# The last output tile of an attention and MLP kernel in two column pieces of 384 and 128

## The chip, the cores and the metric

The kernel runs on one core of one Trainium2 chip. The metric is the time of one execution on the device in microseconds.

## The reference

```python
scores = 0.125 * q @ k_all^T            # 8 batches, 8 heads, 576 queries, 16 beacon + 576 keys, D = 64
a = softmax(causal mask of scores)      # the beacon keys are always seen
x = (a @ v_all) as 4608 tokens x 512
h = x @ w_in                            # 512 -> 2048
g = h * sigmoid(1.702 * h)
out = g @ w_out                         # 2048 -> 512, float32, 4608 x 512
```

## The kernel before

The program is a list of work items, which a small scheduler orders when the program is built. The MLP takes the tokens in nine groups of 512. The second matrix product of a group makes four output tiles of 128 tokens by 512 columns. Each is 16 accumulating matmuls, a copy from PSUM to SBUF, and a store:

```python
def mlp2(g, mt):
    o = psu.tile([P, DMODEL], F32, tag="u", name="u")
    ou[(g, mt)] = o
    for nt in range(NNT):                                  # 16
        nc.tensor.matmul(o[:, :], gts[g][:, nt, mt * P : (mt + 1) * P], w2t[:, nt, :],
                         start=(nt == 0), stop=(nt == NNT - 1))

def mlp2_out(g, mt, eng):
    osb = sp.tile([P, DMODEL], F32, tag="osb", name="osb")
    ...                                                    # nc.scalar.copy or nc.vector.tensor_copy
    ou[(g, mt)] = osb

def mlp2_store(g, mt):
    t0 = g * GT + mt * P
    nc.sync.dma_start(out=out[t0 : t0 + P, :], in_=ou[(g, mt)][:, :])
```

The pool psu has four buffers in PSUM, the pool of osb three in SBUF.

The softmax here doesn't subtract the row's maximum and nothing guards it: scores larger than these inputs give would overflow.

## Time and profile before

| | before |
|---|---|
| time | 367.96 us (three runs, 367.85 to 367.99) |
| span of the profiled run | 366.9 us |
| start of the last tile's first matmul, called T | 359.55 us |
| last copy starts | T + 3.65 |
| last store issued | T + 4.37 |
| its last completion count | T + 6.38 |
| end of the span | T + 7.31 |

T and the times from it are read off the trace's records of single instructions, packets and completion counts. A completion count is what a store adds to a semaphore when a part of it is done: 16 counts for each store here. A store has landed with its last count, and the time from the end of its last data packet to that count is called its receipt. Stores take eight such semaphores in turn, numbered 0 to 7. At the end of the program SP, the engine that issues the stores, waits for them in a fixed order: these are the closing waits.

Two stretches, before and after the end of the last matmul, show how little there is to win:

```profile
core 0: us, PE busy (x) PEld busy (x) DVE busy (x) ACT busy (x) POOL busy (x), PEclk, DMA share, GB/s
359.30:363.20 3.90, 3.87 (x18) 1.57 (x16) 0.69 (x1) 0.00 (x0) 0.00 (x0) 1.00 0.18 67
363.20:367.00 3.80, 0.00 (x0) 0.00 (x0) 0.69 (x1) 0.00 (x0) 0.00 (x0) 0.96 0.18 69
```

In the first, TensorE is busy all the time at the full granted clock (PEclk 1.00). In the second, 3.7 us of the whole 367, one copy is all the work that a compute engine does; the rest is the store and the end of the program. The change works on that second stretch.

### The profile page before, as it was taken

The numbers are of one execution on the slowest core, as the hardware profiler recorded it, in microseconds if no ns is written. First come the engines' busy times: TensorE is split into PE (matmuls) and PEld (weight loads), VectorE is DVE, ScalarE is ACT, GpSimd is POOL, SyncE is SP. The second block draws the span as 40 slices with busy tenths as digits, with TensorE's granted clock in tenths as the row PEclk, the third lists the DMA queues.
The fourth block names the chain that finished last, engine by engine and source line by source line (L and its number), as shares of the span: only waits on it lengthen the run. The fifth ranks groups of instructions, "written<-read, shape, count | busy, mean of one in ns | idle before, by whom it ended". The sixth has DMA issues, their size and how long they took to land.

```text
span 366.9 us, 6133 instructions
## 1 busy us (share of the span) xinstructions
PE 353.5 (96%) x2349; PEld 176.8 (48%) x2349; DVE 249.3 (68%) x421; ACT 228.0 (62%) x335; POOL 153.1 (42%) x264
## 2 busy tenths in 40 slices
PE   7689999999999999999999999999999999999995
PEld 3355444444444444544445864544444454444442
DVE  5547499999999986999599949981995183010021
ACT  4669787648765776677857675677658734616200
POOL 9678567593368245743376236710430010000000
PEclk9969999999999999999999999999999999999999
DMA  9999999994689645894479537921100011000012
GB/s 143 148 206 189 188 237 234 220 113 100 191 235 175 129 130 145 129 171 132 126 111 142 164 112 144 134 88 32 59 30 29 2 57 57 2 29 29 30 57 86
DMA packets 69788, 43.41 MB, mean 118 GB/s; under 512 B 42624, under 2 KB 62080, under 8 KB 69760
## 3 DMA queue, kind: packets, MB, share of 16 engines
q0 software_dynamic: 49152, 18.19, 48.6%
q1 hardware_dynamic: 20400, 24.55, 21.2%
q8 instruction: 18, 0.29, 0.3%
q10 hardware_dynamic: 208, 0.29, 0.3%
q14 instruction: 10, 0.08, 0.1%
HBM read 44.60 MB, written 16.61 MB: 167 GB/s over the span
## 4 chain that ended last, share of the span: by engine, by line
PE 79%; DVE 11%; DMA 3%; ACT 3%; POOL 2%; issue 1%; DVEq 0%; POOLq 0%
PE u L516 34%; PE u L538 30%; PE u L401 7%; PE s L331 6%; DMA g<-in_q_dram 3%; ACT E L344 2%; DVE zt L470 2%; DVE O L459 2%; DVE xT L489 2%; DVE t L262 1%; PE u L430 1%; POOL vb L221 1%; DVE rz L480 1%; DVE osb L551 1%; PE u L190 1%
## 5 line engine op out<-in xcount | busy, mean ns | idle before, releaser
L344 ACT ACTIVATE E<-s 128x1024 f16<-128x1024 f32 (+3 forms) x128 | 103.4, 865 | 48.7 <-PE s L331 46.5
L538 PE MATMUL u<-w,g 128*128 128x512 f16 x576 | 129.2, 379 | 0.6 <-DVE O L459 0.4
L516 PE MATMUL u<-xT,w 128*128 128x512 f16 (+1 forms) x640 | 126.0, 358 | 0.0
L528 ACT ACTIVATE g<-u 128x512 f16<-128x512 f32 x144 | 85.2, 597 | 42.8 <-PE u L516 42.5
L367 POOL TENSOR_SCALAR_AFFINE_SELECT E<-E 128x256 f16<-128x256 f16 (+2 forms) x148 | 63.8, 450 | 83.8 <-ACT E L344 83.6
L516 PEld LDWEIGHTS <-w 128*128 128x128 f16 x640 | 62.1, 98 | 61.3 <-issue 0.9
L538 PEld LDWEIGHTS <-g 128*128 128x128 f16 x576 | 54.5, 98 | 65.4 <-issue 3.6
L551 DVE COPY osb<-u 128x512 f32<-128x512 f32 x30 | 20.5, 683 | 65.2 <-PE u L538 65.0
L459 DVE COPY O<-u 128x240 f32<-128x240 f32 (+1 forms) x84 | 34.8, 440 | 24.4 <-PE u L401 22.1
L262 POOL COPY t<-sq 128x576 f16<-128x576 f16 x21 | 26.7, 1274 | 49.2 <-DVE sq L253 42.8
L401 PE MATMUL u<-E,vb 128*128 128x240 f16 x392 | 46.8, 266 | 0.2
L489 DVE TENSOR_TENSOR xT<-O,rz 64x576 f16<-64x576 f32 x56 | 44.3, 790 | 0.8
L470 DVE STREAM_TRANSPOSE zt<-O 64x576 f32<-64x576 f32 x56 | 43.1, 770 | 1.4
L401 PEld LDWEIGHTS <-vb 128*128 128x128 f16 x392 | 32.2, 98 | 17.4 <-issue 8.0
L331 PE MATMUL s<-qT,kT 64*128 64x80 f16 (+5 forms) x384 | 37.1, 285 | 2.8 <-ACT E L344 1.8
L253 DVE STREAM_TRANSPOSE sq<-n 128x576 f16<-128x576 f16 x48 | 34.9, 747 | 6.6 <-DMA n<-in_k_dram 6.3
L221 POOL DMA_DIRECT2D vb<-in_v_dram x40 | 34.4, 866 | 3.6 <-DMA w<-in_moe_w_in_dram 2.6
L262 DVE COPY t<-sq 128x576 f16<-128x576 f16 x27 | 27.6, 1021 | 0.3
L331 PEld LDWEIGHTS <-kT 64*128 64x128 f16 x384 | 13.3, 94 | 27.4 <-issue 19.4
L480 DVE STREAM_TRANSPOSE rz<-rt 128x576 f32<-128x576 f32 x32 | 24.4, 763 | 0.6
L459 ACT COPY O<-u 128x336 f32<-128x336 f32 (+1 forms) x28 | 10.7, 428 | 2.9 <-PE u L401 2.7
L1043 PE MATMUL u<-wu 128*128 128x512 f16 x29 | 10.5, 456 | 1.3 <-DVE wu L1036 1.3
(44 smaller groups left out, 124.5 us busy)
## 6 DMA issues: line engine op xcount, KB each, us to landing
out_dram<-osb SPq DMA_DIRECT2D x36, 256.0 KB, 2.1
d<-t SPq DMA_DIRECT2D x12, 296.0 KB, 2.6
kT<-d SPq DMA_DIRECT2D x12, 296.0 KB, 3.4
n<-in_k_dram POOLq DMA_DIRECT2D x12, 288.0 KB, 4.8
n<-in_q_dram POOLq DMA_DIRECT2D x12, 288.0 KB, 5.9
d<-t SPq DMA_DIRECT2D x12, 288.0 KB, 2.4
qT<-d SPq DMA_DIRECT2D x12, 288.0 KB, 3.2
vb<-in_v_dram POOLq DMA_DIRECT2D x24, 128.0 KB, 5.7
```

The source lines that it names most:

```text
L221: nc.gpsimd.dma_start(out=vb[r : r + hi - lo, j, :, 0:D], in_=v[b, :, lo:hi, :].rearrange("h n d -> n h d"),)
L262: copy[eng](out=tqk[(b, g, w)][:, e, o : o + S].rearrange("p (r t) -> p r t", t=TPP), in_=sqs[(b, g, w)][:, :, e, :].rearrange("p t r -> p ...
L331: nc.tensor.matmul(sc[:, x, o : o + e - a], kT[r : r + 64, p, j * P : (j + 1) * P], qT[r : r + 64, p, a:e], start=True, stop=True,)
L344: nc.scalar.activation(out=Es[i][:, :, choff[ci] : choff[ci] + w], in_=scs[(i, ci)][:, :, 0:w], func=AFT.Exp, scale=0.125,)
L367: nc.gpsimd.affine_select(out=blk, in_=blk, compare_op=ALU.is_ge, fill=0.0, base=mc, pattern=[[0, 2], [1, w]], channel_multiplier=-1,)
L401: nc.tensor.matmul(u[:, lo:hi], vb[0:kw, j, :, :].rearrange("r h c -> r (h c)")[:, o : o + 2 * D], E[0:kw, x, col : col + hi - lo], start= ...
L459: copy[eng](out=Os[i][:, x, AQ[half] : AQ[half + 1]], in_=avu[(i, x, half)][:, :])
L470: nc.vector.transpose(zst[i][0][64 * x : 64 * x + 64, :, :], Os[i][64 * (1 - x) : 64 * (1 - x) + 64, x, :])
L489: vec[eng].tensor_tensor(out=xT[r : r + 64, p, c : c + S], in0=Os[i][r : r + 64, x, :], in1=zst[i][2][r : r + 64, :], op=ALU.mult,)
L516: nc.tensor.matmul(u[:, o : o + w], w1t[:, kp, nt * P : (nt + 1) * P], xT[:, kp, m : m + w], start=(kp == 0), stop=(kp == NKP - 1),)
L528: nc.scalar.activation(out=gts[g][:, nt, :], in_=hu[(g, nt)][:, :], func=AFT.Gelu_apprx_sigmoid)
L538: nc.tensor.matmul(o[:, :], gts[g][:, nt, mt * P : (mt + 1) * P], w2t[:, nt, :], start=(nt == 0), stop=(nt == NNT - 1),)
```

## The change

The aim is to hide most of the last tile's copy and store under its own matmuls. The tile becomes a piece of 384 columns and one of 128; while the second piece is multiplied, the first is copied and stored, so only a short copy and a small store remain after the last matmul. The core of the diff (the rest passes `a` and `e` through and orders the second piece after the first; `e - a` is a piece's width, and both pieces are copied by DVE):

```diff
+    TAIL = (0, 384, DMODEL)
+
+    def mlp2(g, mt, a=0, e=DMODEL):
+        o = psu.tile([P, e - a], F32, tag="u", name="u")
 ...
-                w2t[:, nt, :],
+                w2t[:, nt, a:e],
 ...
+        osb = sp.tile([P, e - a], F32, tag="osb", name="osb")
+        copy[eng](out=osb[:, :], in_=ou[(g, mt, a)][:, :])
 ...
-        nc.sync.dma_start(out=out[t0 : t0 + P, :], in_=ou[(g, mt)][:, :])
+        nc.sync.dma_start(out=out[t0 : t0 + P, a:e], in_=ou[(g, mt, a)][:, :])
 ...
-        for n in range(GT // P):
+        for n, a, e in [
+            (n, a, e)
+            for n in range(GT // P)
+            for a, e in (zip(TAIL, TAIL[1:]) if (g, n) == (NG - 1, GT // P - 1) else [(0, DMODEL)])
+        ]:
 ...
-                dict(ACT=0.6, DVE=0.66), 0, k1 - 0.3, lambda eng, g=g, n=n: mlp2_out(g, n, eng),
-                [m], alloc=o_,
+                dict(ACT=0.6, DVE=0.66) if e - a == DMODEL else dict(DVE=0.66), 0, k1 - 0.3,
+                lambda eng, g=g, n=n, a=a, e=e: mlp2_out(g, n, eng, a, e), [m], alloc=o_,
```

More of the change, by code (lines that the diff above doesn't have):

```diff
@@ L532 @@
     ou = {}
-    def mlp2(g, mt):
-        o = psu.tile([P, DMODEL], F32, tag="u", name="u")
-        ou[(g, mt)] = o
+    TAIL = (0, 384, DMODEL)
+    def mlp2(g, mt, a=0, e=DMODEL):
+        o = psu.tile([P, e - a], F32, tag="u", name="u")
+        ou[(g, mt, a)] = o
         for nt in range(NNT):
@@ L544, in mlp2, with mlp2_out, mlp2_store @@
             )
-    def mlp2_out(g, mt, eng):
-        osb = sp.tile([P, DMODEL], F32, tag="osb", name="osb")
-        if eng == "ACT":
-            nc.scalar.copy(out=osb[:, :], in_=ou[(g, mt)][:, :])
-        else:
-            nc.vector.tensor_copy(out=osb[:, :], in_=ou[(g, mt)][:, :])
-        ou[(g, mt)] = osb
-    def mlp2_store(g, mt):
+    def mlp2_out(g, mt, eng, a=0, e=DMODEL):
+        osb = sp.tile([P, e - a], F32, tag="osb", name="osb")
+        copy[eng](out=osb[:, :], in_=ou[(g, mt, a)][:, :])
+        ou[(g, mt, a)] = osb
+    def mlp2_store(g, mt, a=0, e=DMODEL):
         t0 = g * GT + mt * P
-        nc.sync.dma_start(out=out[t0 : t0 + P, :], in_=ou[(g, mt)][:, :])
+        nc.sync.dma_start(out=out[t0 : t0 + P, a:e], in_=ou[(g, mt, a)][:, :])
     class Work:
@@ L923 @@
         prev = gl
-        for n in range(GT // P):
-            u_, o_ = Buf("u"), Buf("osb")
-            k1 = k0 + 1 + n
-            m = Work("PE", 3.46, k1, lambda g=g, n=n: mlp2(g, n), gl + W2, alloc=u_)
+        for n, a, e in [
[3 more added lines that the diff above has]
+        ]:
+            u_, o_ = Buf("u"), Buf("osb")
+            k1 = k0 + 1 + n + 0.1 * (a > 0)
+            m = Work(
+                "PE", NNT * (e - a) / 2370, k1, lambda g=g, n=n, a=a, e=e: mlp2(g, n, a, e),
+                gl + W2, alloc=u_, after=[m2s[(g, n)]] if a else (),
+            )
             m2s[(g, n)] = m
@@ L930 @@
             oc = Work(
-                dict(ACT=0.6, DVE=0.66), 0, k1 - 0.3, lambda eng, g=g, n=n: mlp2_out(g, n, eng),
-                [m], alloc=o_,
+                dict(ACT=0.6, DVE=0.66) if e - a == DMODEL else dict(DVE=0.66), 0, k1 - 0.3,
+                lambda eng, g=g, n=n, a=a, e=e: mlp2_out(g, n, eng, a, e), [m], alloc=o_,
             )
             use(u_, oc)
-            ot = Work("SP", 0.73, k1, lambda g=g, n=n: mlp2_store(g, n), [oc], dma=0.9)
+            ot = Work(
+                "SP", 0.73, k1, lambda g=g, n=n, a=a, e=e: mlp2_store(g, n, a, e), [oc], dma=0.9
+            )
             use(o_, ot)
```

## The prediction

> **What bounds the kernel now.** I read the page first, then the chain of waits in the last 22 us, the timeline of the last 4.6 us, the last store's packets, and the end-of-program instructions. From the page:
>
> ```profile
> span 366.9 us, 6133 instructions
> PE 353.5 (96%) x2349; PEld 176.8 (48%) x2349; DVE 249.3 (68%) x421; ACT 228.0 (62%) x335; POOL 153.1 (42%) x264
> PE 79%; DVE 11%; DMA 3%; ACT 3%; POOL 2%; issue 1%; DVEq 0%; POOLq 0%
> ```
>
> TensorE is busy 96% of the span and 79% of the chain that ended last: everything ahead of the last tile is matmul work that this change leaves alone. Only the end can move. The chain there, and the timeline (columns: start, length, engine, line, work, count, idle before):
>
> ```profile
> 3 pieces in order of time: start us, us, what
> 344.82 18.36 PE u L538 x85
> 363.18 0.02 issue
> 363.20 0.69 DVE osb L551
> ...
> 362.57 0.59 PE L538 MATMUL u<-w,g 128*128 128x512 f16 x2
> 363.20 0.69 DVE L551 COPY osb<-u 128x512 f32<-128x512 f32 x1 [2.76 <-PE u L538]
> 363.92 0.33 SPq L556 DMA_DIRECT2D out_dram<-osb  x1
> ```
>
> Nothing overlaps the tail: last matmul, a copy of 512 columns (0.69), a store of 256 KB issued at 363.92, then 2.9 us without any engine's work until 366.9. The packets of that store, in the window from 364.7 to 365.6:
>
> ```profile
> DMA  0097279499949997799499479949999772230000
> q1 hardware_dynamic: 144, 0.26, 76.7%
> ```
>
> 76.7% of 16 engines over 0.9 us is 11.0 us for 128 packets of 2 KB: 86 ns each, 8 per engine, so 0.69 us of moving on each engine. The raw records put the first packet at 364.75, which is 0.83 us after the issue, and the last one's end at 365.58; the completion counts arrive until 365.93. So a store is 0.83 of start, 0.83 of moving (8 x 85 ns, and 0.15 because the engines don't start together), and 0.35 of receipt: 2.0 us. What comes after is the end-of-program line, for SP in two windows (364.26 to 364.8, and 364.8 to 366.0):
>
> ```profile
> L1073 SPq EVENT_SEMAPHORE  x8: 28/28/28, 364.3 to 364.7; - x8
> ...
> L1073 SPq EVENT_SEMAPHORE  x1: 28/28/28, 365.9 to 365.9; - x1
> ```
>
> SP waits in nine instructions: eight pass at once, 61 ns apart (364.300 to 364.731 in the records), and the ninth waits for the store and passes at 365.95. From there to 366.85 are barriers of all engines, 0.9 us, which don't depend on the change.
>
> **What the skill says.** The Trainium skill, "DMA: Bandwidth & Descriptors", section on the anatomy of one DMA, fits a DMA issued by GpSimd as 2.0 us plus bytes over 436 GB/s, most of the fixed part the write receipt. This trace has 2.0 us in total for 256 KB issued by SP, so the fixed part here is nearer 1.2 us; the page's slope would give 0.45 us for 192 KB less, and the trace 0.48 (below). "VectorE: DVE Perf Modes", section on the TRN2 errata, gives a copy from PSUM as 120 plus the columns, in cycles of 0.96 GHz: 658 ns for 512, where the trace has 683; I use the trace. "TensorE: Matmul & The Clock Gate", "Back-to-back issue gap", gives about 81 ns for each matmul of 128 columns in a stream with weight loads; the trace disagrees (below). "Perfetto Trace Analysis", "Identifying Dependency Chains", says that an instruction with several waits may get EventSemaphore instructions ahead of it; the nine above are of that kind.
>
> **The change part by part.** The instruction orders of both programs are the same on every engine up to the last tile: the warm-up matmuls, the choice of ACT or DVE for each copy, all stay. The last tile's 16 matmuls of 512 become 16 of 384 and then 16 of 128; its one copy and one store become two. I count from T, the start of the tile's first matmul (359.55 in the records).
>
> Matmuls. In the records, matmuls of 512 columns follow each other at 216 ns and those of 256 at 109: columns at 2.4 GHz plus 2.5 ns. Those of 384 should then take 162.5. For 128 columns the attention part has the answer: where a matmul of 128 stands before one of 336, with a full weight load for the second, the next starts 56 ns later, and after one of 80 columns 40 ns later. The loads (98 ns each in the profile) start as the previous matmul does and are pipelined. So 16 x 162.5 = 2.60 and 16 x 56 = 0.90: 3.50 against 3.46, +0.04.
>
> First copy. The copy started 416 ns after the start of the last matmul of 512; I take off the streaming difference (columns / 2.4). Piece A's copy can start at T + 2.80. Its length from these groups:
>
> ```profile
> L551 DVE COPY osb<-u 128x512 f32<-128x512 f32 x30 | 20.5, 683 | 65.2 <-PE u L538 65.0
> L459 DVE COPY O<-u 128x240 f32<-128x240 f32 x47 | 18.6, 396 | 22.4 <-PE u L401 22.1
> L459 DVE COPY O<-u 128x336 f32<-128x336 f32 x37 | 18.2, 496 | 2.1
> ```
>
> From 240 to 336 columns is 100 ns, 1.04 per column. So 384 columns take 0.55 and 128 take 396 - 112 x 1.04 = 279 ns. Copy A ends at T + 3.35 and its store is issued at T + 3.38, while the matmuls of piece B still run: all hidden.
>
> Last copy. Piece B's last matmul starts at T + 2.60 + 15 x 0.056 = T + 3.44, its copy 0.256 later at T + 3.70 (before: T + 3.65). DVE has been free for 0.35. It ends at T + 3.98 where it was T + 4.35: -0.37. SP has issued store A by T + 3.72, so store B goes at T + 4.01 rather than T + 4.37: -0.36 in all.
>
> Last store. 128 rows of 512 bytes. Packets in the records: 81 to 85 ns for 2 KB, 65 for 1.5 KB, 51 for 1152 bytes, so 20 ns per 512 bytes on about 5: some 25 ns, an estimate. Eight are 0.20 us instead of 0.68: -0.48. Store A's packets run from T + 4.21, and 8 x 65 = 0.52 on each engine end 0.1 us before B's arrive 0.83 after its issue; no queueing. Start and receipt stay. B lands at about T + 5.55, A well before, against T + 6.38 before: -0.84 so far.
>
> The closing waits. The built programs show what SP waits for in the nine instructions: after one of GpSimd's DMAs alone, hardware DMA semaphores 0 to 7 in that order, each paired with something long done. Stores take the eight in turn. Before, the last store holds number 7: the ninth wait, nothing behind it. The extra store moves the last one on to number 0: the second wait. The seven others come only after it has landed, all satisfied, at 61 ns each: 7 x 61 = +0.43.
>
> Sum: +0.04 - 0.41 (copy) - 0.48 + 0.43 = -0.42 us, or 367.96 - 0.42 = 367.54.
>
> **Rivals.** (1) The closing waits cost nothing extra (SP gets through them otherwise than in program order): the full -0.84 shows, 367.1. For it speaks that the profile doesn't show which semaphore each wait names, so the order is the program's word alone; against it, the even 61 ns of eight passed waits. (2) The matmuls of 128 are bound by weight loads, at the page's 81 ns or at the 98 of the load records: +0.4 to +0.7 on the path, so between 367.9 and 368.2. Against it are the 56 and 40 ns steps, though the trace has no long run of 128. (3) The small store lands no sooner, because start and receipt rule or rows of 512 bytes write slowly, perhaps behind store A: without the 0.48 the sum is +0.06, 368.0. Against it, the packet times fall with size down to 256 bytes (15 to 31 ns). (4) Copy B waits for DVE or for a buffer: its three osb buffers were last stored two tiles earlier and had landed, so no.
>
> **Range and chances.** All these stay within 1 us of 368, and 2% is 7.4 us, so nothing named here can reach the threshold. Repeats of before spread 0.14 us, and another chip may differ by some tenths. The prediction is 367.54, with 367.1 to 368.0 eight times in ten; faster by over 2% 0.005, within 2% 0.985, slower 0.01.
>
> **What would show it.** In the profile of the changed kernel: last-tile matmuls 3.50 us from first start, with the 128s 56 ns apart (81 or more: rival 2); a last copy of 128x128 of about 0.28; last issue 0.36 us earlier after T; a store landing in about 1.5 us rather than 2.0 (rival 3 otherwise); and on SP, in the end-of-program line, one wait before the landing and eight within 0.43 us from it (rival 1: the barriers follow at once). The prediction is wrong if the last copy is not the last to release a store, or if anything ahead of the last tile moves.

## The result, and the profile after

The changed kernel took 367.87 us (median of six runs, 367.64 to 368.47), the kernel before 367.98 in the same rounds (six, 367.39 to 368.43). The ratio is 1.0 with a 95% interval of 0.9987 to 1.0013. The ratios here and below are not the ratios of the medians, and the means of all listed times give slightly other ones for e1 and e10 (0.9985 and 0.9979). The time is the same within 2%, and the rounds can't tell 0.3 us from nothing. The trace can.

The chain of the changed kernel's last microseconds, and then the timeline (start, length, engine, line, work, count, idle before):

```profile
343.89 19.26 PE u L541 x105
363.16 0.02 issue
363.18 0.29 DVE osb L551
```

```profile
362.29 0.56 DVE L551 COPY osb<-u 128x384 f32<-128x384 f32 x1 [1.91 <-PE u L541]
362.87 0.96 SPq L556 DMA_DIRECT2D out_dram<-osb  x2
363.18 0.29 DVE L551 COPY osb<-u 128x128 f32<-128x128 f32 x1 [0.34 <-PE u L541]
```

The copy of 384 columns starts 0.87 us before the last matmul's end (363.16), so it is hidden, and DVE then idles 0.34 us until the second piece is ready: the second copy waits for TensorE and nothing else. The tail copy is 0.29 us instead of 0.69. The line of SP covers both stores: issued at 362.87 and, in the records, at 363.50.

SP's closing waits, in a window up to 365.0 and one after it (the columns of durations in ns, then the first and last start in us):

```profile
L1082 SPq EVENT_SEMAPHORE  x1: 28/28/28, 363.9 to 363.9; - x1
...
L1082 SPq EVENT_SEMAPHORE  x8: 27/28/28, 365.2 to 365.6; - x8
```

The prediction showed eight and then one for the kernel before. Here it is one, and then eight: the last store's wait is the second of nine, and seven more follow it.

Both tails in the records, counted from each kernel's T (359.55 before, 359.49 after), with the prediction's own step beside them:

| from T, us | before | after | difference | predicted difference |
|---|---|---|---|---|
| last copy starts | 3.654 | 3.694 | +0.040 | +0.04 |
| last store issued | 4.373 | 4.012 | -0.361 | -0.36 |
| its last data packet ends | 6.032 | 5.208 | -0.824 | -0.84 |
| its last completion count | 6.383 | 5.674 | -0.709 | -0.84 |
| last of the nine waits passes | 6.399 | 6.120 | -0.279 | -0.42 |
| span ends | 7.306 | 7.026 | -0.280 | -0.42 |

The tail is 0.28 us shorter, 0.08% of the time. A warning goes with the page of the changed kernel:

```profile
span 366.5 us, 6169 instructions
...
PE 83%; DMA 7%; DVE 3%; ACT 3%; issue 2%; POOL 0%; SPq 0%; DVEq 0%; ACTq 0%
```

The chain's shares moved (DVE had 11%, DMA 3%), though ahead of T the instruction orders are the same and DVE's busy time is 249.0 us against 249.3. Where two engines release a wait at nearly the same moment, the chain can go back through either. Such a shift is not a gain.

### The profile page after: what moved, and what is told of

Same layout as the page of the kernel before. It is cut to its first block, busy times and chain, and to the rows that moved or that the text cites. A ratio compares the mean times of both kernels' runs of the same rounds, so it can differ in the third digit from the quotient of the medians.

```text
span 366.5 us, 6169 instructions
## 1 busy us (share of the span) xinstructions
PE 353.7 (97%) x2365; PEld 177.8 (49%) x2365; DVE 249.0 (68%) x422; ACT 228.4 (62%) x335; POOL 152.7 (42%) x264
## 4 chain that ended last, share of the span: by engine, by line
PE 83%; DMA 7%; DVE 3%; ACT 3%; issue 2%; POOL 0%; SPq 0%; DVEq 0%; ACTq 0%
PE u L516 34%; PE u L541 34%; PE u L401 9%; PE s L331 6%; DMA g<-in_k_dram 4%; ACT E L344 2%; DMA O<-in_beacon_k_dram 2%; DMA osb<-in_beacon_k_dram 1%; DVE xT L489 1%; DVE zt L470 1%; DVE O L459 1%; DVE osb L551 0%; ACT L344 0%; POOL E L367 0%; ACT bk L136 0%
## 5 line engine op out<-in xcount | busy, mean ns | idle before, releaser
L541 PE MATMUL u<-w,g 128*128 128x512 f16 (+2 forms) x592 | 129.3, 373 | 0.6 <-DVE O L459 0.4
L541 PEld LDWEIGHTS <-g 128*128 128x128 f16 x592 | 55.5, 98 | 64.8 <-issue 3.6
L551 DVE COPY osb<-u 128x512 f32<-128x512 f32 (+2 forms) x31 | 20.6, 666 | 64.6 <-PE u L541 64.4
```

## The experiments

There were ten experiments, two of which repeat a kernel (e5 the change, e10 e1); each was correct except the one meant to be wrong. Single runs of one core have the state "unknown", so I use only their tails; the matmuls of 512 columns just ahead of T keep their 216 ns in each. The measure is T to the end of the span.

| run | T to issue | to last count | to end | time against before, ratio (95% interval) |
|---|---|---|---|---|
| before | 4.37 | 6.38 | 7.31 | |
| the change | 4.01 | 5.67 | 7.03 | 1.0 (0.9987 to 1.0013) |
| e1: change, last store on semaphore 7 | 4.01 | 5.59 | 6.51 | 0.9986 (0.9973 to 1.0) |
| e2: before, last store on semaphore 0 | 4.37 | 6.39 | 7.75 | 1.0014 (1.0001 to 1.0027) |
| e3: split matmuls and copies, one store | 4.01 | 6.01 | 6.93 | single run |
| e4: change without the first store (wrong) | 4.01 | 5.68 | 6.60 | single run |
| e5: the change again | 4.01 | 5.68 | 7.03 | 0.9988 (0.9975 to 1.0002) |
| e6: e1 with 256 and 256 | 4.15 | 5.87 | 6.79 | single run |
| e7: e1 with 448 and 64 | 4.30 | 6.08 | 7.00 | single run |
| e8: e7, last piece by ACT | 3.94 | 6.08 | 7.00 | 0.9987 (0.9974 to 0.9999) |
| e9: change, last store on semaphore 3 | 4.01 | 5.65 | 6.81 | single run |
| e10: e1 again | 4.01 | 5.59 | 6.52 | 0.9975 (0.9961 to 0.9989) |

**e1, the closing waits put right.**

```diff
-        nc.sync.dma_start(out=out[t0 : t0 + P, a:e], in_=ou[(g, mt, a)][:, :])
+        r = P // 8 if (g, mt) == (NG - 2, 3) else P
+        for y in range(0, P, r):
+            nc.sync.dma_start(out=out[t0 + y : t0 + y + r, a:e], in_=ou[(g, mt, a)][y : y + r, :])
```

> The changed kernel, with the store of an earlier tile (group 7, fourth tile, issued 17 us before the end) cut into eight row pieces, so that seven more hardware DMAs put the last store on completion semaphore 7 again; the rest is the same. I measure from T, the start of the last tile's first matmul, to the span's end: 7.306 us before, 7.026 with the change. Theory (the order of the closing waits gives back 0.43 us): only the ninth wait stays open until the store lands, so T to end is 7.026 - 0.43 = 6.60, and over the pair of the same chip the time is about 0.7 us (0.19%) below before. Rival (the gain stayed small for another reason, and the closing waits only look serial): T to end stays at 7.0, whatever number the store holds.

T to end is 6.51 us, 0.51 less than the change. SP's closing waits in this run, up to 364.5 and after it:

```profile
L1084 SPq EVENT_SEMAPHORE  x8: 28/28/28, 363.4 to 364.3; - x8
...
L1084 SPq EVENT_SEMAPHORE  x1: 28/28/28, 364.6 to 364.6; - x1
```

Eight ahead of the landing, one at it. Of the 0.51, the waits are 0.43: in the change the last wait passed 0.45 us after the last count, here 0.02. The other 0.08 is an earlier last count, taken up under e4 and e10. The median is 367.37 us against 368.07 before. The rival falls.

**e2, the same shift without the split.** In the kernel before, the store of the same earlier tile is cut in two.

```diff
-        nc.sync.dma_start(out=out[t0 : t0 + P, :], in_=ou[(g, mt)][:, :])
+        r = P // 2 if (g, mt) == (NG - 2, 3) else P
+        for y in range(0, P, r):
+            nc.sync.dma_start(out=out[t0 + y : t0 + y + r, :], in_=ou[(g, mt)][y : y + r, :])
```

> The kernel before, unsplit, with the store of the same earlier tile cut into two row pieces: one more hardware DMA, so the last store moves from completion semaphore 7 to 0. Theory: copy and store of the last tile as before, landing at T + 6.38, then seven waits after it: T to end 7.306 + 0.43 = 7.73, time 0.43 us (0.12%) above before. Rival: no difference, 7.31.

T to end is 7.75. Up to 365.7, and after it:

```profile
L1075 SPq EVENT_SEMAPHORE  x1: 28/28/28, 364.2 to 364.2; - x1
...
L1075 SPq EVENT_SEMAPHORE  x8: 27/28/28, 365.8 to 366.3; - x8
```

Issue and landing are those of the kernel before within 0.01 us; only the seven waits came behind the landing, +0.44. Cutting in two a store that was issued 17 us before the end cost 0.41 us in the medians: 368.48 against 368.07, with an interval just above 1.

**e9, a point between.** As e1, with `P // 4`.

> The change with the earlier tile's store in four row pieces instead of one: three more hardware DMAs, so the last store holds semaphore 3, whose wait is the fifth of nine. Theory (waits in program order, 61 ns each): four waits after the landing, 0.25 us instead of 0.43, so T to end is 7.03 - 0.18 = 6.85, with 4 waits before the landing and the landing's wait fifth. Rival (number 7 is special for another reason, the others cost the same): 7.03.

T to end is 6.81 us. Up to 364.3, and after it:

```profile
L1084 SPq EVENT_SEMAPHORE  x4: 28/28/28, 363.2 to 364.1; - x4
...
L1084 SPq EVENT_SEMAPHORE  x5: 27/28/28, 364.5 to 364.7; - x5
```

The landing's wait is the fifth and four follow, as expected. From last count to last wait it is 0.45 us with semaphore 0, 0.26 with 3 and 0.02 with 7. The order of the waits is shown as the cause of what is lost after the landing.

**e3, the copy half alone.** Both copies write one tile, and one store of 256 KB follows.

```diff
-        osb = sp.tile([P, e - a], F32, tag="osb", name="osb")
-        copy[eng](out=osb[:, :], in_=ou[(g, mt, a)][:, :])
-        ou[(g, mt, a)] = osb
+        osb = ou[(g, mt)] if a else sp.tile([P, DMODEL], F32, tag="osb", name="osb")
+        copy[eng](out=osb[:, a:e], in_=ou[(g, mt, a)][:, :])
+        ou[(g, mt)] = osb
 ...
-        nc.sync.dma_start(out=out[t0 : t0 + P, a:e], in_=ou[(g, mt, a)][:, :])
+        if e == DMODEL:
+            nc.sync.dma_start(out=out[t0 : t0 + P, :], in_=ou[(g, mt)][:, :])
```

> Matmuls and copies of the last tile in 384 and 128 columns as in the change, but both copies write one tile and one store of 256 KB follows the second: the copy half of the change alone, last store on semaphore 7. Theory: the issue is 0.36 us earlier than before (T + 4.01), the store takes 2.01 us from issue to landing as before, so T to end is 7.306 - 0.36 = 6.95. Rival (a split copy gains nothing, since the 128-column matmuls or the second copy cost what it saves): 7.3.

Issue at T + 4.01, landing 1.99 later, end at T + 6.93: the copy half is worth 0.38. This kernel lands 0.33 us later than the change and still ends 0.10 us sooner after T: it has one store fewer, so its last one keeps semaphore 7 and the 0.43 of waits stays away.

**e4, the small store by itself.**

```diff
+        if (g, mt, a) == (NG - 1, 3, 0):
+            return
```

> The change without the store of the 384 columns (those outputs are wrong on purpose; one DMA fewer, last store on semaphore 7). In the change the small store took 1.66 us from issue to its last completion count, where I predicted 1.54: last packet's end to last count was 0.47 us, not 0.35. Theory A (it shares the engines or the memory with the first store's writes, which ended 0.3 us earlier): without that store it lands 0.35 after its last packet, 1.54 from issue. Theory B (the receipt of rows of 512 bytes takes longer by itself): still 1.66. T to end is then 7.026 - 0.43 - 0.12 = 6.48 under A, 6.60 under B.

The store landed 1.67 us after its issue, 0.49 after its last packet, and T to end is 6.60: theory B. The first store's writes do not cause the long receipt. Sharing with that store is ruled out; that the size of the rows does it is not yet shown.

**e10, the receipt and the time once more.** The kernel of e1.

> The first experiment's kernel again, for two things. Its last receipt was 0.37 us where three other runs with rows of 512 bytes had 0.46 to 0.49: if the rows' size decides, this run has 0.46 to 0.49 and T to end 6.60; if the extra row pieces or semaphore 7 did it, 0.37 and 6.51 again. And the time: 0.70 to 0.79 us below before by the traces, a ratio near 0.998.

The receipt was 0.385 us (0.37 in e1), and T to end 6.52. So the size of the rows does not decide it alone: rows of 512 bytes had 0.47, 0.47 and 0.49 (change, e5, e4), 0.43 with four row pieces of an earlier store (e9), 0.37 and 0.385 with eight (e1, e10). Semaphore 7 doesn't decide it either, as e4 holds it with 0.49. Nor do eight pieces alone: e7 and e8 have them too, and a receipt of 0.48 (with rows of 256 bytes). Nor does the chip: e1 and e4 ran on the same one. The first of the 16 counts comes at T + 5.412 in the change and at T + 5.415 in e1; only the later ones come later in the change. The cause stays open. The time is 367.57 us against 368.27, ratio 0.9975, clear of 1.

**e5, the change again.** Unedited.

> The changed kernel itself, unedited, so that it stands beside the kernel before and beside the best variant on one chip. By its trace it should gain 7.306 - 7.026 = 0.28 us from T to end, 0.08% of the time. Theory: a ratio near 0.9992, its interval holding 1; the last store's receipt (last packet's end to last completion count) somewhere between the 0.37, 0.47 and 0.49 us of the three runs of it so far. Rival: the gain in the trace is bought back ahead of T, and the ratio is 1.000 or above.

The tail repeats to 0.01 us. The ratio is 0.9988 with 1 inside the interval; 0.9992 lies inside it too, and inside that of the first rounds. The spread of single runs comes from ahead of T: over the twelve traces, T itself lies between 358.81 and 359.63 us, while the tails of equal programs differ by 0.01. A loss ahead of T of a tenth or two could not be seen here; nothing speaks for one.

**e6, pieces of 256 and 256.** The kernel of e1 with `TAIL = (0, 256, DMODEL)`.

> The first experiment's kernel (last store on semaphore 7) with pieces of 256 and 256 columns rather than 384 and 128. Theory (the last piece's copy and rows set the tail): copy 396 + 16 x 1.04 = 413 ns instead of 291, issue T + 4.13 instead of T + 4.01; rows of 1 KB at some 46 ns each, 8 of them, 0.15 us more than rows of 512 bytes; T to end 6.51 + 0.12 + 0.15 = 6.78, give or take 0.1 for the receipt, which would be 0.35 if long receipts belong to rows of 512 bytes alone. Rival (any split gives the same): 6.5.

6.79, as expected: a copy of 424 ns, an issue at T + 4.15, packets of 46 ns. The receipt was 0.38 us.

**e7, pieces of 448 and 64.** The kernel of e1 with `TAIL = (0, 448, DMODEL)`.

> The first experiment's kernel with pieces of 448 and 64 columns. Theory (a smaller last piece runs into new waits): the first copy of 448 columns ends at about T + 3.84 and its store occupies SP until T + 4.20, so the last store is issued at about T + 4.28 instead of T + 4.01 though its own copy is done at T + 4.08; T to end 6.51 + 0.27 - 0.07 (rows of 256 bytes) = 6.7. Rival (smaller is better still, copy 0.07 and rows 0.07 shorter): 6.37. It also shows the pace of matmuls of 64 columns: 29 ns apart if columns alone set it, 40 or more if weight loads do.

The issue came at T + 4.30 as expected, but T to end is 7.00, not 6.7. Set against e1, the first packet came 1.01 us after the issue instead of 0.85, and the receipt was 0.48. The first store's own packets (1792 bytes each) ran until T + 5.48, and the last store's began at T + 5.31. The matmuls of 64 columns stood 29 ns apart.

**e8, SP and DVE taken off the last piece.** As e7, with these two lines more:

```diff
-            nc.sync.dma_start(out=out[t0 + y : t0 + y + r, a:e], in_=ou[(g, mt, a)][y : y + r, :])
+            (nc.scalar if a else nc.sync).dma_start(out=out[t0 + y : t0 + y + r, a:e], in_=ou[(g, mt, a)][y : y + r, :])
-                dict(ACT=0.6, DVE=0.66) if e - a == DMODEL else dict(DVE=0.66), 0, k1 - 0.3,
+                dict(ACT=0.6, DVE=0.66) if e - a == DMODEL else dict(ACT=0.6) if a else dict(DVE=0.66), 0, k1 - 0.3,
```

> As the run before, but the last piece is copied by ACT and its store issued by ACT, so that it waits neither for DVE's long copy nor for SP's issue. Theory: matmuls done as there, ACT's copy of 64 columns 0.21 to 0.23 us from about T + 3.70, issue at about T + 3.95, rows of 256 bytes 0.07 faster than in the first experiment: T to end 6.51 - 0.06 - 0.07 = 6.38, the best so far, 0.9 us (0.25%) below before. Rival (SP and DVE were not what held the last store back): T to end as in the run before, 6.7.

Both were wrong. The issue did move to T + 3.94, and nothing came of it. The timeline of e8, and then its DMA queues in the window from 364.2 to 364.7 (packets, MB, share of 16 engines; q1 is SP's, q10 ACT's):

```profile
362.21 0.62 DVE L551 COPY osb<-u 128x448 f32<-128x448 f32 x1 [2.33 <-PE u L541]
362.67 0.21 ACT L551 COPY osb<-u 128x64 f32<-128x64 f32 x1 [20.16 <-PE u L541]
362.86 0.33 SPq L558 DMA_DIRECT2D out_dram<-osb  x1
362.91 0.37 ACTq L558 DMA_DIRECT2D out_dram<-osb  x1
```

```profile
q10 hardware_dynamic: 144, 0.03, 29.0%
q1 hardware_dynamic: 40, 0.04, 24.7%
```

ACT copies while DVE still does, and its store goes out 0.06 us behind SP's. But all 144 packets of ACT's queue lie at the tail of SP's: the first began at T + 5.30, 1.36 us after its issue, while SP's store was in its last packets. The last completion count came at T + 6.08, within 0.01 us of e7, where the issue was 0.37 us later. So with 448 columns the first store is no longer hidden: for both times of issue, the last store's packets began only as the first's ended, and the end came at the same time. That the first store holds them back is argued from this; no run sent the small store from ACT without a store ahead of it. In the change it is nearly out of the way: its packets end at T + 4.90, and the last store's begin at T + 4.87.

## Why the prediction was right

The time, 367.87 us, lies in the range, and "within 2%" held. Neither says much: the range also holds the 367.98 us of the kernel before, so it would have held with no gain at all. What supports the prediction is the tail, where the forecast of -0.42 was of the right sign and mechanism, and half as large again as the -0.28 measured. Point by point:

- *What bounds the kernel.* Right. The orders ahead of T are the same, and the shortening is all in the tail.
- *Matmuls, +0.04.* Right: 162.5 ns apart at 384 columns, 56 at 128, last copy +0.04. Rival 2, weight loads at 81 or 98 ns, fell here, and e7 with 29 ns at 64 columns buries it.
- *Copies.* Right in place, mis-sized by little: the last is 291 ns, not 279. The issue moved by 0.36 as predicted, and e3 shows that part alone.
- *Last store, -0.48.* This is the term that was mis-sized. The moving was right (packets of 27 ns, and 0.49 us less of it), but "start and receipt stay" was wrong. The receipt took 0.47 us instead of 0.35, and the start 0.855 instead of 0.83; these 0.115 and 0.025 are the 0.14 by which the sum misses. e4 rules out that the first store causes the longer receipt; e1 and e10 with 0.37 and 0.385 show that it isn't a constant of such stores. Its cause is open. The longer start goes with the first store: e4, without it, has 0.834. "No queueing" was thus slightly wrong. The prediction let store A's packets end 0.1 us before B's begin, without the 0.15 us by which the engines start apart; A's last packet ended 0.035 us after B's first began.
- *Closing waits, +0.43.* Right to 0.01 us, and shown by the runs: 0.45, 0.26 and 0.02 us from last count to last wait with the store on semaphore 0, 3 and 7, in both directions (e1, e2). Rival 1 fell. It could have fallen before any run. The prediction says that the profile doesn't show which semaphore each wait names, but only the views leave it out: the single records of the trace do name them. In the kernel before, the nine waits name the stores' eight semaphores in order, and the ninth names the one on which the last store's 16 counts arrive; in the change, those counts arrive on the first of the eight, which the second wait names.
- *Rivals 3 and 4* fell: the store lands 0.71 us sooner after T, and the second copy waits for TensorE alone. Rival 3's transfer "perhaps behind store A" does come true once the pieces are 448 and 64 (e7, e8).

The change therefore earned 0.71 us and gave back 0.43 of it to seven waits that were already satisfied. The version that keeps both, e1, ends 0.79 us sooner after T than the kernel before, and its two sets of rounds gave 0.70 us each in the medians. It is the best of all tried, and still far from 2%.

## What to carry to other kernels

After the last transfer is issued, look at what the program still does in order: a wait for the last thing should be the last wait, and one DMA more or fewer, even far ahead of the end (17 us in e2), can change which one it is. When a tail is cut into pieces, the last piece sets the gain only until the piece before it stops being hidden; check when that one's transfer ends, not only when its issue does. And a change in a 4 us tail of a 368 us kernel is judged from the tail in the trace, counted from a fixed event, because run-to-run scatter ahead of it is larger than the effect.

## What the Trainium skill lacked or had wrong

- No page that I found says what a program's closing waits cost: nine waits in a fixed order, 61 ns for each that is already satisfied, so 0.43 us for seven behind the last landing. "Perfetto Trace Analysis", section "Identifying Dependency Chains", has the extra EventSemaphore instructions, for an instruction that waits on multiple engines, but not that their order at the end can cost 0.43 us.
- "TensorE: Matmul & The Clock Gate", section "Back-to-back issue gap": 81 ns for each matmul of 128 columns and 131 for 512 in a stream with weight loads; its formula N/2.4 + 2.5 is said to hold for an isolated matmul. Here sixteen such pairs of 128 columns ran 56 ns apart, sixteen of 64 columns 29 ns and those of 512 columns 216 ns apart, as that formula gives.
- "VectorE: DVE Perf Modes", section "The TRN2 errata": 120 cycles and, without a perf-mode multiplier, one per column at 0.96 GHz for a copy from PSUM gives 525, 258 and 192 ns for 384, 128 and 64 columns. The runs had 558, 291 and 214.
- "DMA: Bandwidth & Descriptors", section on the anatomy of one DMA: the fit is for GpSimd's path, with most of the fixed 2 us put down to the write receipt. Stores issued by SP took 2.01 us for 256 KB and 1.58 to 1.67 for 64 KB. In the kernel before, 0.83 us passed ahead of the first packet and only 0.35 after the last, and over the runs the receipt varied from 0.35 to 0.49 us.
- Same page, section "Issuing engines are not separate DMA queues": e8 agrees that a second issuing engine saves nothing. ACT's store, issued 0.06 us behind SP's, had its first packet only 1.36 us after its issue. But the page has such DMAs interleave, and here ACT's first packet began at T + 5.30, when 120 of SP's 128 data packets had begun.
